# A projection piece taken undivided, read by two engines at one time, and its words split by GpSimd

## The chip, the cores and the metric

The kernel runs on one core of one Trainium2 chip. A core has TensorE (PE, matmuls), VectorE (DVE), ScalarE (ACT), GpSimd (POOL) and SyncE (SP, which here issues DMAs). They run side by side, each in the order of its own queue, and wait for one another by semaphores. Matmuls write PSUM, which VectorE and ScalarE can read. The metric is the time of one execution in microseconds (us); lower is better.

## The reference

The input `x` is 8 sequences of 4096 tokens with 192 channels. Each token becomes a weighted sum of itself and the six before it, with seven softmax weights for each of 8 heads of 24 channels. What comes out goes through a gated network:

```python
out = np.einsum('hk,bskhg->bshg', w, x_unf)     # the convolution, w = softmax(weight)
x = out.reshape(B * S, D)                       # 32768 x 192
gate = np.maximum(x @ w_gate, 0.0)              # 192 -> 1536
val = x @ w_val                                 # 192 -> 1536
return (gate * val @ w_out).astype(np.float32)  # 1536 -> 192
```

## The kernel before, in words

The sequences are taken in two streams, of four sequences each, which lie on partitions 0 to 63 and 64 to 127. The 4 x 4096 tokens of a stream are cut into 16 units of 1024 tokens, and each unit into two windows of 512. The matmuls are in float16, their sums in float32. The order on every engine is the order in which the code is written out; a framework adds the waits.

Unit `u` goes through these steps.

- **Gate and value** (`gate_val`, L534 to L564): for each window, 12 blocks of 128 features. Each block takes two PSUM tiles (gate, value) of 12 matmuls each (L549). ScalarE takes the Relu of the gate (L560), VectorE multiplies it with the value (L561) into `hT`. PSUM is a pool of four tiles of two banks, taken in turn, so a block can start only when the block two before it has been read.
- **Convolution of the next unit.** The part of 576 tokens is VectorE's: ScalarE gives the first of seven products (`lane_first`, L507), VectorE adds six (`lane_rest`, L521). The other 448 tokens are GpSimd's: products for each tap `k` and channel chunk `c` go into the buffer `prods`, of which there is one; ScalarE makes most of them (L491), VectorE the five in the list `VECTOR` (L493). In the following unit GpSimd adds them up, one add for each tap (`add`, L497).
- **Input of the unit after that**: GpSimd reorders loaded tokens (`lane_turn`, L471), SP issues nine transposes of them (L475), and GpSimd issues the next loads (`lane_load`, L207).
- **Projection** (`project_across`, L706, for units 1 to 14). It is computed transposed, output channels on partitions and tokens along the columns, as three pieces: piece 0 and piece 1 are channels 0 to 127 of the two windows, piece 2 is channels 128 to 191 of both. Each piece holds two streams or windows in the two banks of one PSUM tile. [...] A no-operation in SP's queue (`turn_over`, L671) stands between the turns. The order of the passes is (piece 0, turn 0), (2, 0), (0, 1), (1, 0), (2, 1), (1, 1).
- **Out of PSUM.** A float32 is copied as two 16-bit words, low words and high words apart (`words`, L678, its copies in L679), so that 16-bit DMA transposes can turn the planes. SP writes the planes to a DRAM buffer `held` (L739, L744); in the next unit it issues four transposes from there (`turn_back`, L687) and four writes to the output (`send`, L697).

The last pass, (piece 1, turn 1), is divided into two halves of 256 columns:

```python
cross_pass(1, hs, at[1], 1, done[1], slice(0, half))
words(nc.scalar.copy, pt, at[1], both, 0, half)
cross_pass(1, hs, at[1], 1, None, slice(half, WIN))
words(nc.scalar.copy, pt, at[1], slice(0, 1), half, WIN)
words(nc.vector.tensor_copy, pt, at[1], slice(1, 2), half, WIN)
```

Beside this work VectorE makes three of its five products at the end of `lane_rest` (L857), that is before its `words` copy, and the other two after it (L746).

Of the kernel before, what the change touches and what calls it, by code (L numbers as in the profile page):

```python
# [8 lines left out]
FP = mybir.dt.float32  # L9
F16 = mybir.dt.float16  # L10
I32 = mybir.dt.int32
U16 = mybir.dt.uint16
# [5 lines left out]
def kernel(  # L18
# [12 lines left out]
    nc = tc.nc  # L31

    B, S, D = x.shape
# [8 lines left out]
    WIN = 512  # L42
    NWIN = S // WIN
    SUB = 112
    VECTOR = [(0, 5), (1, 5), (2, 5), (0, 6), (2, 1)]
    FOR_POOL = [(1, 6), (2, 6)]
    GSUB = 5
    DSUB = 104
# [3 lines left out]
    NUNIT = NB * S // UNIT  # L52
# [11 lines left out]
    xpool = ctx.enter_context(tc.tile_pool(name="xpool", bufs=2))  # L64
# [3 lines left out]
    ypool = ctx.enter_context(tc.tile_pool(name="ypool", bufs=1))  # L68
# [4 lines left out]
    psum = ctx.enter_context(tc.tile_pool(name="psum", bufs=4, space=bass.MemoryType.PSUM))  # L73
# [442 lines left out]

    def lane_rest(v, now=len(VECTOR)):
        acc = accs.pop(v)
        for k in range(1, KW):
            for c in range(NCH):  # L520
                nc.vector.scalar_tensor_tensor(  # L521
                    out=xc[v][:, c, 0:LDVE] if k == KW - 1 else acc[:, c, :],
                    in0=shifted(v, c, k, 0),
                    scalar=tap[:, c, k : k + 1],
                    in1=acc[:, c, :],
                    op0=ALU.mult,
                    op1=ALU.add,
                )
        if v + 1 < NUNIT:
            prods[v] = apool.tile([128, KW, NCH, LPOOL], FP, name="prods")  # L530
            for c, k in VECTOR[:now]:
                product(nc.vector, v, c, k)
# [108 lines left out]
                flat[:, q0 : q0 + n],  # L641
            )

    across, planes = {}, {}

    def cross_pass(piece, hs, ps, turn, after, cols=slice(0, WIN)):


        for f in range(NFF):
            for r in range(2):  # L650
                bank = r ^ turn
                for half in range(2):
                    if piece == 2:
                        w, st, d = bank, half, 128
                    else:
                        w, st, d = piece, bank, 64 * half
                    mm = nc.tensor.matmul(  # L657
                        out=ps[64 * half : 64 * half + 64, bank, cols],
                        lhsT=Wo[64 * r : 64 * r + 64, f, d : d + 64],
                        rhs=hs[w][64 * r : 64 * r + 64, f, st, cols],  # L660
                        start=(turn == 0 and f == 0),
                        stop=(turn == 1 and f == NFF - 1),
                        tile_position=(64 * r, 64 * half),
                        skip_group_check=True,
                    )
                    if after is not None:
                        tc.add_manual_dep(mm.ins, after.ins.name, SYNC, reason="same banks, other rows")
                        after = None
        return turn_over(turn, mm)
# [5 lines left out]
        tc.add_manual_dep(done.ins, mm.ins.name, SYNC, reason="first turn over")  # L675
        return done

    def words(copy, pt, ps, banks, t0, t1):  # L678
        copy(  # L679
            out=pt[:, banks, :, t0:t1],  # L680
            in_=ps[:, banks, t0:t1].bitcast(U16).rearrange("p b (t l) -> p b l t", l=2),
        )

    def turn_back(u, i):
        w, st = i // 2, i % 2
        os_ = opool.tile([128, 4, D], FP, name="out_s")
        nc.sync.dma_start_transpose(  # L687
            out=os_[:].bitcast(U16),
            in_=planes[u][w, st].rearrange("c (l t) -> (c l) t", l=2),
        )  # L690
        across[u, i] = os_

    def send(u, i):
        w, st = i // 2, i % 2
        bp, w0 = u * UNIT // S, u * UNIT % S // WIN
        row0 = (bp + NB * st) * S + WIN * (w0 + w)
        nc.sync.dma_start(  # L697
            out=bass.AP(
                tensor=out.tensor,
                offset=out.offset + row0 * D,  # L700
                ap=[[D, 128], [128 * D, 4], [1, D]],
            ),
            in_=across.pop((u, i))[:],
        )

    def project_across(u, hs, work):  # L706
        held = planes[u] = dram.tile([2, 2, D, 2 * WIN], U16, name="held")
        at, done = {}, {}
        back = u - 1 in planes
        both, half = slice(0, 2), WIN // 2  # L710
        for i, turn in [(0, 0), (2, 0), (0, 1), (1, 0), (2, 1), (1, 1)]:
            if turn == 0:
                at[i] = psum.tile([128, 2, 512], FP, name="ps")
                done[i] = cross_pass(i, hs, at[i], 0, None)
                if back:
                    if i == 0:
                        turn_back(u - 1, 3)
                    elif i == 2:
                        send(u - 1, 2)
                    else:  # L720
                        send(u - 1, 3)
                continue
            for c, k in work[(0, 2, 1)[i]]:
                product(nc.scalar, u + 1, c, k)
            pool, name = (ypool, "y") if i == 1 else (xpool, "x_h")
            pt = pool.tile([128, 2, 2, WIN], U16, name=name)
            if i == 1:
                cross_pass(1, hs, at[1], 1, done[1], slice(0, half))
                words(nc.scalar.copy, pt, at[1], both, 0, half)
                cross_pass(1, hs, at[1], 1, None, slice(half, WIN))  # L730
                words(nc.scalar.copy, pt, at[1], slice(0, 1), half, WIN)
                words(nc.vector.tensor_copy, pt, at[1], slice(1, 2), half, WIN)
            else:
                cross_pass(i, hs, at[i], 1, done[i])
                words(nc.scalar.copy, pt, at[i], both, 0, WIN)
            flat = pt[:].rearrange("p b l t -> p b (l t)")
            if i == 2:
                for st in range(2):
                    nc.sync.dma_start(  # L739
                        out=held[:, st, 128:D, :].rearrange("w c e -> c w e"),  # L740
                        in_=flat[64 * st : 64 * st + 64],
                    )
            else:
                nc.sync.dma_start(out=held[i, :, 0:128, :].rearrange("s c e -> c s e"), in_=flat)  # L744
        if u + 2 < NUNIT:
            for c, k in VECTOR[3:]:  # L746
                product(nc.vector, u + 1, c, k)

    def project(u, hs, work, y=None):
# [68 lines left out]
    for u in range(NUNIT):  # L818
        adds = 1 <= u < NUNIT - 1
        if u + 1 < NUNIT:  # L820
            xc[u + 1] = xcpool.tile([128, NCH, UNIT], F16, name="xc")
        if adds:
            add(u, 1)
        hs = []
        if u == 0:
            hs.append(gate_val(0, 0))
        if 0 < u < NUNIT - 1:
            load_rest(lane_turn(u + 1))
        if u - 1 in planes:
            turn_back(u - 1, 0)  # L830
            turn_back(u - 1, 1)
            send(u - 1, 0)
            turn_back(u - 1, 2)
            send(u - 1, 1)
            if u == NUNIT - 1:
                turn_back(u - 1, 3)
                send(u - 1, 2)
                send(u - 1, 3)
        if 0 < u < NUNIT - 2:
            load_rest(lane_load(u + 2))  # L840
        if u == 1:
            for c, k in FOR_POOL:
                product(nc.gpsimd, u, c, k)
        if adds:
            for k in range(2, KW):
                add(u, k)
        while len(hs) < 2:
            hs.append(gate_val(u, len(hs)))
        del xc[u]
        work = [[] for _ in range(4)]  # L850
        if u + 1 < NUNIT:
            begun = lane_first(u + 1)
            if u == 0:
                flat = ypool.tile([128, ROOM], F16, name="y")
                y = flat[:, 0 : GSUB * NCH * 128].rearrange("p (j c s r) -> p j c s r", j=GSUB, c=NCH, s=2)
                load_rest(lane_load(2, begun))
            lane_rest(u + 1, len(VECTOR) if u in (0, NUNIT - 2) else 3)  # L857
        if u + 2 < NUNIT:
            todo = [(c, k) for k in (0, 1, 2, 3, 4, 6) for c in range(NCH)]
            todo = [ck for ck in todo if ck not in VECTOR + (FOR_POOL if u == 0 else [])]  # L860
            cuts = [0, 5, 10, 15, 16] if u == 0 else [0, 10, 16, 16]
            work = [todo[a:b] for a, b in zip(cuts, cuts[1:])]
        if 0 < u < NUNIT - 1:
            project_across(u, hs, work)
        else:
            project(u, hs, work, y if u == 0 else None)
        if u == 0:
            conv_turn(2, y)
# [30 lines left out]
```

## Time and profile before

| | |
|---|---|
| median of three runs | 791.49 us (790.75 to 794.97) |
| the profiled execution | 789.98 us |
| its span, first to last instruction | 788.2 us |
| PE busy | 761.1 us, 97% |
| DVE busy | 706.0 us, 90% |
| ACT busy | 630.3 us, 80% |
| POOL busy | 379.9 us, 48% |
| granted TensorE clock | 1.00 |

A row of a group of instructions gives the line, the engine, the operation, the tiles written and read, the shape and the count, then the busy time and the mean of one in ns, then the idle time of that engine just before them and what ended it. A row of the timeline gives start, duration, engine, line and operation; a bracket gives the idle time before it and the releaser. The line of a helper stands for all who call it: L679 is every copy of `words`, and the tile's name tells which (`x_h` for pieces 0 and 2, `y` for piece 1).

### The profile page before, as it was taken

What the parts mean: (1) busy time and instruction counts of PE and PEld (TensorE: products, weight loads), DVE (VectorE), ACT (ScalarE), POOL (GpSimd) and SP (SyncE); (2) the same over time, 40 slices, a digit from 0 to 9 for tenths busy, and PEclk for the clock granted to TensorE, in tenths of its full rate; (3) what the DMA queues carried; (4) which work ended last, traced back from release to release, by engine and by line L of the source; (5) the groups of instructions that cost most, each with busy time, mean ns of one, the idle gap of its engine ahead of it and who ended that gap; (6) DMA issues with size and microseconds to landing.
All of it is one profiled execution on the core that took longest, in us unless ns stands there. A gap on an engine that the chain in (4) does not pass through costs nothing.

```text
span 788.2 us, 31924 instructions
## 1 busy us (share of the span) xinstructions
PE 761.1 (97%) x14295; PEld 504.5 (64%) x14295; DVE 706.0 (90%) x768; ACT 630.3 (80%) x733; POOL 379.9 (48%) x249
## 2 busy tenths in 40 slices
PE   9999999999999999999999999999999999999998
PEld 4495566666666666666666666666666666666548
DVE  7999989899898998989989899898998989999791
ACT  6787978879788797887978879788797887876672
POOL 8529358092561916619165290753908438081000
PEclk9999999999999999999999999999999999999999
DMA  8969039596594965949769496794969939443732
GB/s 114 131 119 129 2 97 153 158 115 141 121 160 141 108 163 105 152 143 117 164 105 147 138 122 159 105 153 131 144 139 119 161 114 146 125 117 92 174 89 82
DMA packets 231313, 100.42 MB, mean 127 GB/s; under 512 B 185288, under 2 KB 220424, under 8 KB 231176
## 3 DMA queue, kind: packets, MB, share of 16 engines
q1 hardware_dynamic: 189928, 82.71, 52.1%
q0 software_dynamic: 41104, 15.57, 20.5%
q8 instruction: 111, 1.82, 1.0%
q14 instruction: 26, 0.21, 0.1%
q10 hardware_dynamic: 144, 0.10, 0.0%
HBM read 31.48 MB, written 47.19 MB: 100 GB/s over the span
## 4 chain that ended last, share of the span: by engine, by line
PE 67%; ACT 26%; issue 2%; DMA 2%; SPq 2%; POOL 0%; ACTq 0%; DVE 0%; POOLq 0%
PE ps L549 59%; ACT prods L491 15%; ACT x_h L679 6%; PE ps L657 4%; ACT acc L507 3%; PE ps L578 3%; ACT y L679 2%; SPq L475 1%; DMA out_s<-held 1%; PE ps L627 1%; DMA x_h<-in_x_dram 0%; PE ps L369 0%; POOL x_p L471 0%; ACTq L491 0%; POOL x_h L133 0%
## 5 line engine op out<-in xcount | busy, mean ns | idle before, releaser
L561 DVE TENSOR_TENSOR hT<-gr,ps 128x1024 f16<-128x1024 f16 (+1 forms) x386 | 467.8, 1216 | 30.3 <-ACT gr L560 6.1
L560 ACT ACTIVATE gr<-ps 128x1024 f16<-128x1024 f32 (+1 forms) x386 | 393.4, 1020 | 104.2 <-PE ps L549 103.2
L497 POOL TENSOR_TENSOR prods<-prods 128x1344 f32<-128x1344 f32 x70 | 212.9, 3042 | 312.5 <-DVE prods L493 309.1
L549 PE MATMUL ps<-xc,Wv 64*64 64x512 f16 (+1 forms) x4320 | 322.8, 376 | 0.3
L549 PE MATMUL ps<-xc,Wg 64*64 64x512 f16 (+1 forms) x4320 | 322.8, 376 | 0.0
L657 PE MATMUL ps<-hT,Wo 64*64 64x512 f16 (+1 forms) x4704 | 223.4, 346 | 22.1 <-ACT y L679 22.1
L549 PEld LDWEIGHTS <-Wv 64*64 64x64 f16 (+1 forms) x4320 | 154.3, 105 | 97.3 <-issue 4.6
L549 PEld LDWEIGHTS <-Wg 64*64 64x64 f16 (+1 forms) x4320 | 157.0, 106 | 89.2 <-issue 0.4
L657 PEld LDWEIGHTS <-Wo 64*64 64x64 f16 x4704 | 157.1, 107 | 88.6 <-issue 24.8
L521 DVE SCALAR_TENSOR_TENSOR acc<-x_r,tap,acc 128x576 f32<-128x576 f16 x225 | 165.3, 815 | 0.0
L491 ACT ACTIVATE prods<-x_r,tap 128x448 f32<-128x448 f16 x222 | 127.4, 662 | 0.0
L679 ACT COPY x_h<-ps 128x2048 uint16<-128x2048 uint16 x28 | 51.9, 1852 | 8.7 <-PE ps L657 8.7
L207 POOL DMA_DIRECT2D x_e<-in_x_dram x58 | 46.9, 818 | 15.4 <-ACT acc L507 11.6
L471 POOL COPY x_p<-x_e 128x960 f16<-128x960 f16 (+1 forms) x58 | 50.5, 912 | 0.5 <-DMA x_e<-in_x_dram 0.4
L497 POOL TENSOR_TENSOR xc<-prods 128x1344 f16<-128x1344 f32 x14 | 42.5, 3038 | 1.1
L679 ACT COPY y<-ps 128x1024 uint16<-128x1024 uint16 (+1 forms) x28 | 22.4, 801 | 22.4 <-PE ps L657 22.4
L679 DVE COPY y<-ps 128x512 uint16<-128x512 uint16 x14 | 9.7, 692 | 30.6 <-ACT y L679 30.6
L521 DVE SCALAR_TENSOR_TENSOR xc<-x_r,tap,acc 128x576 f16<-128x576 f16 x45 | 34.1, 816 | 0.0
L507 ACT ACTIVATE acc<-x_r,tap 128x576 f32<-128x576 f16 x45 | 31.4, 765 | 0.0
L493 DVE TENSOR_SCALAR prods<-x_r,tap 128x448 f32<-128x448 f16 x70 | 27.7, 450 | 0.0
L578 PE MATMUL ps<-Wo,hT 64*128 64x192 f16 x576 | 24.6, 243 | 0.0
L578 PEld LDWEIGHTS <-hT 64*128 64x128 f16 x576 | 23.9, 94 | 0.5
(61 smaller groups left out, 80.4 us busy)
## 6 DMA issues: line engine op xcount, KB each, us to landing
out_dram<-out_s SPq DMA_DIRECT2D x62, 384.0 KB, 3.9
held<-x_h SPq DMA_DIRECT2D x14, 512.0 KB, 2.8
held<-x_h SPq DMA_DIRECT2D x28, 256.0 KB, 3.2
held<-y SPq DMA_DIRECT2D x14, 512.0 KB, 3.3
x_e<-in_x_dram POOLq DMA_DIRECT2D x34, 192.0 KB, 7.5
x_e<-in_x_dram POOLq DMA_DIRECT2D x24, 240.0 KB, 5.2
x_r<-x_p SPq DMA_TRANSPOSE x131, 5.5
out_s<-held SPq DMA_TRANSPOSE x56, 4.5
```

The lines of the kernel that those rows point to most:

```text
L207: first = nc.gpsimd.dma_start(out=xe[:, j0 + start : j0 + n, st, :, :].rearrange("p j c r -> p j (c r)"), in_=bass.AP(tensor=x.tensor, off ...
L471: nc.gpsimd.tensor_copy(out=xp[:, j0 : j0 + n, :, st, :], in_=xe[:, j0 : j0 + n, st, :, :])
L491: engine.activation(out=out, in_=in_, func=ACTF.Copy, scale=scale)
L497: nc.gpsimd.tensor_tensor(out=pr[:, 0] if k < KW - 1 else xc[v + 1][:, :, LDVE:UNIT], in0=pr[:, 0], in1=pr[:, k], op=ALU.add,)
L507: nc.scalar.activation(out=accs[v][:, c, :], in_=shifted(v, c, 0, 0), func=ACTF.Copy, scale=tap[:, c, 0:1],)
L521: nc.vector.scalar_tensor_tensor(out=xc[v][:, c, 0:LDVE] if k == KW - 1 else acc[:, c, :], in0=shifted(v, c, k, 0), scalar=tap[:, c, k : k ...
L549: nc.tensor.matmul(out=pss[i][m : m + M, st, :], lhsT=W[64 * st : 64 * st + 64, c, 128 * f + m : 128 * f + m + M], rhs=xcb[64 * st : 64 * ...
L560: nc.scalar.activation(out=gr[:, sts], in_=pss[0][:, sts], func=ACTF.Relu)
L561: nc.vector.tensor_tensor(out=h[:, f, sts], in0=gr[:, sts], in1=pss[1][:, sts], op=ALU.mult)
L578: mm = nc.tensor.matmul(out=outs[q], lhsT=h[64 * r : 64 * r + 64, f, st, 128 * q : 128 * (q + 1)], rhs=Wo[64 * r : 64 * r + 64, f, :], sta ...
L657: mm = nc.tensor.matmul(out=ps[64 * half : 64 * half + 64, bank, cols], lhsT=Wo[64 * r : 64 * r + 64, f, d : d + 64], rhs=hs[w][64 * r : 6 ...
L679: copy(out=pt[:, banks, :, t0:t1], in_=ps[:, banks, t0:t1].bitcast(U16).rearrange("p b (t l) -> p b l t", l=2),)
```

## The change

- The last pass is no longer divided: it runs over all 512 columns. `cross_pass` loses its column argument and takes, in `ps`, a place for each bank.
- Piece 1 takes two PSUM tiles, not one. The first stream lies in bank 0 of one tile, the second in bank 1 of the other. A unit's projection so takes four PSUM tiles, not three.
- Its two streams are copied as float32 into one tile `raw` of the pool `xpool`, 512 columns by ScalarE and 512 by VectorE; nothing is split into words there. `raw` is a third tenant of the two `x_h` buffers.
- In the next unit, after the reordering of `lane_turn`, GpSimd copies `raw` to the `y` tile as split words (2048 words a partition), and SP then writes the planes to `held`: this write moves from the end of a unit to a place behind the nine transposes of the next.
- The list `VECTOR` begins with (2, 1), which was last, and two products, not three, are made before the copy out of PSUM (`NOW`), three after it.

```diff
-    VECTOR = [(0, 5), (1, 5), (2, 5), (0, 6), (2, 1)]
+    VECTOR = [(2, 1), (0, 5), (1, 5), (2, 5), (0, 6)]
+    NOW = 2
...
                     mm = nc.tensor.matmul(
-                        out=ps[64 * half : 64 * half + 64, bank, cols],
+                        out=ps[bank][64 * half : 64 * half + 64],
                         lhsT=Wo[64 * r : 64 * r + 64, f, d : d + 64],
-                        rhs=hs[w][64 * r : 64 * r + 64, f, st, cols],
+                        rhs=hs[w][64 * r : 64 * r + 64, f, st, :],
...
-    def words(copy, pt, ps, banks, t0, t1):
-        copy(
-            out=pt[:, banks, :, t0:t1],
-            in_=ps[:, banks, t0:t1].bitcast(U16).rearrange("p b (t l) -> p b l t", l=2),
-        )
+    def words(copy, pt, src):
+        copy(out=pt[:], in_=src[:].bitcast(U16).rearrange("p b (t l) -> p b l t", l=2))
+
+    def keep(u, i, pt):
+        flat = pt[:].rearrange("p b l t -> p b (l t)")
+        if i < 2:
+            nc.sync.dma_start(
+                out=planes[u][i, :, 0:128, :].rearrange("s c e -> c s e"), in_=flat
+            )
+            return
+        for st in range(2):
+            nc.sync.dma_start(
+                out=planes[u][:, st, 128:D, :].rearrange("w c e -> c w e"),
+                in_=flat[64 * st : 64 * st + 64],
+            )
...
             if turn == 0:
-                at[i] = psum.tile([128, 2, 512], FP, name="ps")
+                tiles[i] = [psum.tile([128, 2, 512], FP, name="ps") for _ in range(1 + (i == 1))]
+                at[i] = [tiles[i][-n][:, n, :] for n in range(2)]
                 done[i] = cross_pass(i, hs, at[i], 0, None)
...
+            cross_pass(i, hs, at[i], 1, done[i])
             if i == 1:
-                cross_pass(1, hs, at[1], 1, done[1], slice(0, half))
-                words(nc.scalar.copy, pt, at[1], both, 0, half)
-                cross_pass(1, hs, at[1], 1, None, slice(half, WIN))
-                words(nc.scalar.copy, pt, at[1], slice(0, 1), half, WIN)
-                words(nc.vector.tensor_copy, pt, at[1], slice(1, 2), half, WIN)
+                raw = xpool.tile([128, 2, WIN], FP, name="x_h")
+                nc.scalar.copy(out=raw[:, 0, :], in_=at[1][0])
+                nc.vector.tensor_copy(out=raw[:, 1, :], in_=at[1][1])
+                raws[u] = raw
             else:
-                cross_pass(i, hs, at[i], 1, done[i])
-                words(nc.scalar.copy, pt, at[i], both, 0, WIN)
+                pt = xpool.tile([128, 2, 2, WIN], U16, name="x_h")
+                words(nc.scalar.copy, pt, tiles[i][0])
+                keep(u, i, pt)
         if u + 2 < NUNIT:
-            for c, k in VECTOR[3:]:
+            for c, k in VECTOR[NOW:]:
                 product(nc.vector, u + 1, c, k)
...
         if u - 1 in planes:
+            pt = ypool.tile([128, 2, 2, WIN], U16, name="y")
+            words(nc.gpsimd.tensor_copy, pt, raws.pop(u - 1))
+            keep(u - 1, 1, pt)
             turn_back(u - 1, 0)
...
-            lane_rest(u + 1, len(VECTOR) if u in (0, NUNIT - 2) else 3)
+            lane_rest(u + 1, len(VECTOR) if u in (0, NUNIT - 2) else NOW)
```

More of the change, by code (lines that the diff above doesn't have):

```diff
@@ L642, in whole_half, with cross_pass @@
             )
-    across, planes = {}, {}
-    def cross_pass(piece, hs, ps, turn, after, cols=slice(0, WIN)):
+    across, planes, raws = {}, {}, {}
+    def cross_pass(piece, hs, ps, turn, after):
         for f in range(NFF):
@@ L706, in project_across @@
     def project_across(u, hs, work):
[L707 to L710, printed above, removed]
+        planes[u] = dram.tile([2, 2, D, 2 * WIN], U16, name="held")
+        tiles, at, done = {}, {}, {}
         for i, turn in [(0, 0), (2, 0), (0, 1), (1, 0), (2, 1), (1, 1)]:
             if turn == 0:
-                at[i] = psum.tile([128, 2, 512], FP, name="ps")
+                tiles[i] = [psum.tile([128, 2, 512], FP, name="ps") for _ in range(1 + (i == 1))]
+                at[i] = [tiles[i][-n][:, n, :] for n in range(2)]
                 done[i] = cross_pass(i, hs, at[i], 0, None)
-                if back:
+                if u - 1 in planes:
                     if i == 0:
                         turn_back(u - 1, 3)
-                    elif i == 2:
-                        send(u - 1, 2)
                     else:
-                        send(u - 1, 3)
+                        send(u - 1, 2 + (i == 1))
                 continue
@@ L724, in project_across @@
                 product(nc.scalar, u + 1, c, k)
-            pool, name = (ypool, "y") if i == 1 else (xpool, "x_h")
-            pt = pool.tile([128, 2, 2, WIN], U16, name=name)
+            cross_pass(i, hs, at[i], 1, done[i])
             if i == 1:
-                cross_pass(1, hs, at[1], 1, done[1], slice(0, half))
-                words(nc.scalar.copy, pt, at[1], both, 0, half)
-                cross_pass(1, hs, at[1], 1, None, slice(half, WIN))
-                words(nc.scalar.copy, pt, at[1], slice(0, 1), half, WIN)
-                words(nc.vector.tensor_copy, pt, at[1], slice(1, 2), half, WIN)
-            else:
-                cross_pass(i, hs, at[i], 1, done[i])
-                words(nc.scalar.copy, pt, at[i], both, 0, WIN)
[L736 to L744, printed above, removed]
+                raw = xpool.tile([128, 2, WIN], FP, name="x_h")
+                nc.scalar.copy(out=raw[:, 0, :], in_=at[1][0])
+                nc.vector.tensor_copy(out=raw[:, 1, :], in_=at[1][1])
+                raws[u] = raw
+            else:
+                pt = xpool.tile([128, 2, 2, WIN], U16, name="x_h")
+                words(nc.scalar.copy, pt, tiles[i][0])
+                keep(u, i, pt)
         if u + 2 < NUNIT:
-            for c, k in VECTOR[3:]:
+            for c, k in VECTOR[NOW:]:
                 product(nc.vector, u + 1, c, k)
```

## The prediction

> **What bounds the kernel now.** I began with the page: busy shares, the granted clock, then the costliest groups with the idle time before them.
>
> ```profile
> span 788.2 us, 31924 instructions
> PE 761.1 (97%) x14295; PEld 504.5 (64%) x14295; DVE 706.0 (90%) x768; ACT 630.3 (80%) x733; POOL 379.9 (48%) x249
> ...
> L657 PE MATMUL ps<-hT,Wo 64*64 64x512 f16 (+1 forms) x4704 | 223.4, 346 | 22.1 <-ACT y L679 22.1
> ```
>
> TensorE (PE) is busy 97% of the span, and nearly all of the rest is one wait: 22.1 us in which a projection matmul (L657) stands until ScalarE (ACT) has done its `y` copy (L679). So I went to the timeline where a unit's projection meets the next unit. Each row is start, duration, engine, line, operation.
>
> ```profile
> 331.37 14.46 PE L657 MATMUL ps<-hT,Wo 64*64 64x512 f16 x288
> 331.88 2.10 ACT L507 ACTIVATE acc<-x_r,tap 128x576 f32<-128x576 f16 x3
> 333.16 11.02 DVE L521 SCALAR_TENSOR_TENSOR acc<-x_r,tap,acc 128x576 f32<-128x576 f16 x15
> 333.88 5.69 ACT L491 ACTIVATE prods<-x_r,tap 128x448 f32<-128x448 f16 x10
> ...
> 344.10 2.27 DVE L521 SCALAR_TENSOR_TENSOR xc<-x_r,tap,acc 128x576 f16<-128x576 f16 x3
> 344.59 1.85 ACT L679 COPY x_h<-ps 128x2048 uint16<-128x2048 uint16 x1
> 346.28 1.18 DVE L493 TENSOR_SCALAR prods<-x_r,tap 128x448 f32<-128x448 f16 x3
> 346.34 1.01 ACT L679 COPY y<-ps 128x1024 uint16<-128x1024 uint16 x1
> ...
> 347.40 1.50 PE L657 MATMUL ps<-hT,Wo 64*64 64x256 f16 x48 [1.58 <-ACT y L679]
> 348.71 0.84 PE L549 MATMUL ps<-xc,Wg 64*64 64x512 f16 x12
> 348.95 0.59 ACT L679 COPY y<-ps 128x512 uint16<-128x512 uint16 x1 [1.60 <-PE ps L657]
> 349.57 0.69 DVE L679 COPY y<-ps 128x512 uint16<-128x512 uint16 x1 [2.11 <-ACT y L679]
> 349.60 1.02 ACT L560 ACTIVATE gr<-ps 128x1024 f16<-128x1024 f32 x1
> ...
> 350.18 0.81 DVE L493 TENSOR_SCALAR prods<-x_r,tap 128x448 f32<-128x448 f16 x2
> ...
> 350.90 1.22 DVE L561 TENSOR_TENSOR hT<-gr,ps 128x1024 f16<-128x1024 f16 x1
> ...
> 351.30 0.84 PE L549 MATMUL ps<-xc,Wg 64*64 64x512 f16 x12
> 352.17 0.84 PE L549 MATMUL ps<-xc,Wv 64*64 64x512 f16 x12
> ```
>
> The last piece is projected in two column halves. PE does the first, ending at 345.83, then waits 1.58 us because ACT reads that half out of the same PSUM tile from 346.34 to 347.35; only then does the second half run. There is a second, smaller loss: the tile of 12 matmuls that starts at 351.30 is followed by one at 352.17, 0.87 us later instead of about 0.65 (the stage's 31.31 us, below, over 48 tiles). That is the third feature block waiting for the PSUM buffer of the first, which VectorE (DVE) frees at the end of its product at 350.90 + 1.22.
>
> The busy time by stage (length, then PE, its weight loads, DVE, ACT, POOL, and the granted clock, 1.00):
>
> ```profile
> 331.37:348.71 17.34, 15.76 (x340) 11.28 (x336) 16.02 (x23) 15.98 (x23) 0.00 (x0) 1.00 0.40 113
> 348.71:380.02 31.31, 31.29 (x585) 20.34 (x580) 28.76 (x26) 24.56 (x25) 24.92 (x14) 1.00 1.01 141
> ```
>
> So a unit is 17.34 us of projection and 31.31 us of gate and value.
>
> **The change, part by part.**
>
> *Undivided last pass.* What a whole pass costs is read by cutting the window after one, two and five passes:
>
> ```profile
> 331.37 2.79 PE L657 MATMUL ps<-hT,Wo 64*64 64x512 f16 x48
> 331.37 5.38 PE L657 MATMUL ps<-hT,Wo 64*64 64x512 f16 x96
> 331.37 13.15 PE L657 MATMUL ps<-hT,Wo 64*64 64x512 f16 x240
> ```
>
> Each pass adds 2.59 us; the 0.20 us over is the drain of the last matmuls. Six whole passes take 15.54 us, and the next unit would start at 346.91 instead of 348.71: **1.80 us saved** (the wait of 1.58, the drain before it 0.20, and 0.02 of splitting). That needs nobody else to be late at 346.91, so I take each candidate from the rows above.
> - DVE's last write of the next `xc` ends at 344.10 + 2.27 = 346.37. Slack 0.54 us.
> - ACT's copy of the second piece ends at 344.59 + 1.85 = 346.44; its buffer goes to the first value tile, at 346.91 + 0.65 = 347.56. Slack 1.1 us.
> - The two raw copies replace the three `y` copies. 512 elements take ACT 0.59 and DVE 0.69 us in those rows. They start when the pass has drained, 346.91 + 0.20 + 0.05 (348.90 to 348.95 now) = 347.16; DVE has by then done its two products (1.18 x 2/3 after 346.28 is 347.07). ACT ends at 347.75, DVE at 347.85. Their buffers go to the second feature block, at 346.91 + 1.30 = 348.21. Slack 0.35 us, the smallest.
> - ACT starts its first Relu 0.89 us after the unit's start (349.60 against 348.71), here 347.80; the raw copy is done 0.05 us before.
>
> *The stall in the third block.* DVE now does the raw copy and three products, not two, ahead of its first product of gate and value. By the rows, a copy moves it on by 0.61 us (349.57 to 350.18) and a product by 0.36 (350.18 to 350.90 is two): 347.16 + 0.61 + 1.08 = 348.85, 1.94 us after the unit's start against 2.19 now. Its product then ends at 346.91 + 3.16, and the third block's value tile is due at 346.91 + 3.24. So that stall (0.22 us) just goes; between 0 and 0.22 I take 0.22, since the Relu that the product also waits for (347.80 + 1.02) is as early.
>
> *GpSimd (POOL).* It gets one new copy of 2048 two-byte elements a unit, and starts each unit earlier. Its rows in two units,
>
> ```profile
> 302.51 3.04 POOL L497 TENSOR_TENSOR prods<-prods 128x1344 f32<-128x1344 f32 x1 [23.11 <-DVE prods L493]
> ...
> 326.02 3.04 POOL L497 TENSOR_TENSOR xc<-prods 128x1344 f16<-128x1344 f32 x1
> ...
> 351.16 3.04 POOL L497 TENSOR_TENSOR prods<-prods 128x1344 f32<-128x1344 f32 x1 [22.10 <-DVE prods L493]
> 354.14 3.46 POOL L471 COPY x_p<-x_e 128x960 f16<-128x960 f16 x4
> ...
> 373.66 3.04 POOL L497 TENSOR_TENSOR xc<-prods 128x1344 f16<-128x1344 f32 x1
> ```
>
> and, by groups, with the mean of one in ns behind the bar and the busy time:
>
> ```profile
> L471 POOL COPY x_p<-x_e 128x960 f16<-128x960 f16 x30 | 28.8, 988 | 0.3 <-DMA x_e<-in_x_dram 0.3
> ...
> L493 POOL TENSOR_SCALAR prods<-x_r,tap 128x448 f32<-128x448 f16 x2 | 2.8, 1432 | 0.0
> ```
>
> Its first add waits for DVE's product (2, 1), which is now the last of the five and moves to the first: it can start at about 346.8, the unit's start, not 2.45 us after it. From 351.16 to 376.70 POOL needs 25.5 us; from 302.51 to 329.06, in a unit that begins a sequence of the input, 26.5. What it must be done by: ACT overwrites the single `prods` buffer 2.51 us into the next projection (333.88), which is 31.08 + 2.51 = 33.6 us after the unit's start. That leaves 8.1 us for the new copy, or 7. At the rate of its copies (988 ns for 960) it takes 2.1 us, at that of its slowest row (1432 ns for 448) 6.5 us. The operation is a copy, so I take 2.1; either is covered, at no cost. If the cover were gone, each us over 7 costs PE one.
>
> [...]
>
> *DVE beside POOL.* More POOL work lies beside DVE. DVE's product in the 12.5 us with POOL adding, and in the 4 us with POOL idle:
>
> ```profile
> L561 DVE TENSOR_TENSOR hT<-gr,ps x11: 1220/1222/1222, 312.6 to 325.5; 128x1024 f16<-128x1024 f16 x11
> ...
> L561 DVE TENSOR_TENSOR hT<-gr,ps x4: 1221/1221/1222, 328.1 to 332.0; 128x1024 f16<-128x1024 f16 x4
> ```
>
> No difference, so nothing is charged. [...]
>
> *Queues.* The write of the third piece to DRAM leaves SP at the boundary and stands behind the nine transposes of the next unit, with a wait for POOL's copy; behind it are the four transposes back and the sends.
>
> ```profile
> 356.08 14.65 SPq L475 DMA_TRANSPOSE x_r<-x_p  x9
> ...
> 378.01 0.53 SPq L697 DMA_DIRECT2D out_dram<-out_s  x1
> ```
>
> and by DMA, with the median us from issue to landing:
>
> ```profile
> held<-x_h SPq DMA_DIRECT2D x14, 512.0 KB, 2.8
> ```
>
> The transposes end at 370.7, 22 us into the unit; POOL's copy would be done by 3.0 + 3.5 + 6.5 = 13. The write adds 0.4 us of issue and lands some 3 us later, before the third transpose back (376). SP's next duty to PE is the end of the projection's first pass, 380.02 + 2.59 = 382.6, 4 us after its last send. Cost 0, and if SP came later than that, PE would wait by as much. The raw tile takes a buffer of the `x_h` pair, whose first piece is issued at 341.4 and lands 2.8 us later, 3 us before 347.16: 0.
>
> **The sum.** 1.80 + 0.22 = 2.02 us at 13 boundaries; a unit would be 48 tiles of 0.6475 and six passes, 31.08 + 15.54 = 46.62 us with PE never waiting. Unit 14 has neither products nor the second stall:
>
> ```profile
> 720.49 14.46 PE L657 MATMUL ps<-hT,Wo 64*64 64x512 f16 x288
> ...
> 737.95 0.82 PE L549 MATMUL ps<-xc,Wg 64*128 64x512 f16 x6
> ```
>
> 17.46 us, of which 0.1 is the switch to wider tiles that stays: 1.8 saved. 13 x 2.02 + 1.8 = 28.1 us. The profiled execution took 789.98 us (span 788.2 and 1.8 around it), so 761.9; the median of the runs is 1.5 above the profiled one, so **763 us**.
>
> **Rivals.**
> - *The wait only moves.* For it: now DVE's `y` copy starts only when ACT's ends (2.11 <-ACT y). If the raw copies also went one behind the other, DVE's would end at 347.75 + 0.69 = 348.44, 0.25 us past need, and its first product at 348.44 + 1.0 + 1.2 = 350.65, some 0.5 past it. Against: the copies read separate tiles and write separate halves, and both wait for the same earlier ACT instruction. 13 x 0.5 to 0.75 us comes back: 769 to 773.
> - *GpSimd becomes the bound (slower).* Over 7 us for its copy, ACT's products start late; 0.54 us of that is slack, and 2.02 us the gain, so from about 9.5 us (4.6 ns an element) the kernel is slower. At 11 us, 13 x 1.5 = 19 us: 811. For it: two-byte elements four bytes apart, a form that the trace lacks. Against: the rows give 1.0 to 3.2 ns. From 6.3 us, POOL's last add would also reach into L521 (333.16, 31.08 + 1.79 after the start); if an L521 waited for a whole add, PE would lose 3.04 - 0.54 = 2.5 us, 0.48 over the gain: 13 x 0.48 more than 790, 796; I give that 0.01 of this rival's chance. [...]
> - *Nothing gained.* The granted clock falls once PE has no gaps: 4% would eat it all, 790. Against: 1.00 in both windows above, one of them 31 us with PE busy throughout.
>
> **How the numbers follow.** Forecast 759 to 768 (the low end is the sum without the median's 1.5 us and with 0.2 us a boundary for drains counted too long; the high end keeps the third block's stall, 2.9 us, and 0.15 us a boundary): 0.78. Moved wait: 0.10. Nothing gained: 0.05. Slower: 0.07. Faster is the first two, 0.88. A half per cent, 4 us, the spread of the three runs before (790.75 to 794.97), is about what a measurement can tell from no change. The range, 759 to 773, takes the forecast and the moved wait.
>
> **What would show it.** Right: no wait of L657 for a copy, 46.6 us from unit to unit, raw copies of 0.59 and 0.69 us starting together, POOL's first add at the unit's start, its new copy of 2 to 6.5 us, PE busy over 99%. Wrong: idle time before L549's first blocks put down to DVE or ACT copies, the new GpSimd copy over 7 us, L521 over 815 ns, or a granted clock under 1.

## The result and the profile after

The changed kernel takes 830.61 us (median of four runs, 829.84 to 832.17) against 791.12 us of the kernel before: 4.9% slower, ratio 1.0492 with a 95% interval of 1.0453 to 1.0531. The forecast was 763 us.

The page of the changed kernel, in the lines that answer to those of before:

```profile
span 828.1 us, 30624 instructions
PE 781.6 (94%) x13623; PEld 493.2 (60%) x13623; DVE 750.8 (91%) x768; ACT 616.8 (74%) x719; POOL 413.7 (50%) x263
...
PEclk9999999999999998999999999998999999999999
...
L494 DVE TENSOR_SCALAR prods<-x_r,tap 128x448 f32<-128x448 f16 x70 | 72.6, 1088 | 0.0
```

and its list of waits:

```profile
PE ps L550 <- DVE hT L562: 42.4, 13, 3.3
```

The wait of the projection for a copy is gone, as meant. In its place the gate and value matmuls wait 42.4 us for VectorE's product, 13 times, once at each boundary but the last. And one group has changed its duration: VectorE's products for the convolution (L494, before L493) take 1088 ns on average, not 450. The instruction is the same one.

The timeline of one boundary, in the columns of the prediction's:

```profile
411.71 3.44 PE L658 MATMUL ps<-hT,Wo 64*64 64x512 f16 x60
412.14 2.27 DVE L522 SCALAR_TENSOR_TENSOR xc<-x_r,tap,acc 128x576 f16<-128x576 f16 x3
...
414.33 0.81 DVE L494 TENSOR_SCALAR prods<-x_r,tap 128x448 f32<-128x448 f16 x2
...
414.92 3.11 POOL L498 TENSOR_TENSOR prods<-prods 128x1344 f32<-128x1344 f32 x1 [24.19 <-DVE prods L494]
414.95 0.84 PE L550 MATMUL ps<-xc,Wg 64*64 64x512 f16 x12
415.24 0.69 DVE L737 COPY x_h<-ps 128x512 f32<-128x512 f32 x1
415.27 0.59 ACT L736 COPY x_h<-ps 128x512 f32<-128x512 f32 x1 [0.79 <-ACT x_h L680]
...
415.84 4.62 DVE L494 TENSOR_SCALAR prods<-x_r,tap 128x448 f32<-128x448 f16 x3
...
417.54 0.84 PE L550 MATMUL ps<-xc,Wg 64*64 64x512 f16 x12
417.97 3.94 POOL L472 COPY x_p<-x_e 128x960 f16<-128x960 f16 x4
...
420.38 2.33 DVE L562 TENSOR_TENSOR hT<-gr,ps 128x1024 f16<-128x1024 f16 x2
421.64 1.35 PE L550 MATMUL ps<-xc,Wv 64*64 64x512 f16 x12 [3.25 <-DVE hT L562]
...
422.71 1.56 PE L550 MATMUL ps<-xc,Wg 64*64 64x512 f16 x12
...
425.26 0.85 PE L550 MATMUL ps<-xc,Wg 64*64 64x512 f16 x12
```

Up to 415.84 everything is as forecast: the next unit follows the projection at once, and the two raw copies run side by side in 0.69 and 0.59 us. Then the three products behind the raw copy take 4.62 us in place of 1.1. The line's own view for this stretch has their spread (shortest, median and longest of the five, in ns; two of them stand ahead of the raw copy):

```profile
L494 DVE TENSOR_SCALAR prods<-x_r,tap x5: 449/1167/2440, 414.3 to 419.3; 128x448 f32<-128x448 f16 x5
```

The first of the three, 2440 ns, ends at 418.28, just behind the end of GpSimd's add (414.92 + 3.11 = 418.03); the other two, 1167 ns each, lie beside GpSimd's reorder copies, which take about as long one by one (3.94 for four). So VectorE's first product of gate and value starts at 420.38 and not at 416.9, and the value tile due at 417.54 + 0.65 = 418.19 starts at 421.64.

What follows the wait is a second loss, seen in the windows view (length, PE busy, granted clock):

```profile
421.64:425.20 3.56, 3.56 (x36) 0.53 0.37 74
```

The mean granted clock of the stretch is 0.53: for 3.4 us of it the clock is 0.5, and a tile of 12 matmuls takes about 1.28 us. By the trace's record of the clock this happens at all 13 boundaries, for 3.41 us at eleven of them and for 6.8 us at two.

A unit so takes 51.75 us (the chain of waits has projections that start at 399.61 and 451.36): the forecast's 46.62, 3.45 us of lateness (421.64 - 418.19) and the 1.68 us that are left, which the half clock explains (half of 3.41 is 1.71). 13 x 5.13 = 66.7 us on the forecast's 761.9 is 828.6; the profiled execution took 829.84. The two units with 6.8 us at half clock are longer, 53.0 us (294.81 to 347.83 in the chain of waits).

### The profile page after: what moved, and what is told of

Its sections match the earlier page's. It is cut to its first block, busy times and chain, and to the rows that moved or that the text cites. A ratio compares the mean times of both kernels' runs of the same rounds, so it can differ in the third digit from the quotient of the medians.

```text
span 828.1 us, 30624 instructions
## 1 busy us (share of the span) xinstructions
PE 781.6 (94%) x13623; PEld 493.2 (60%) x13623; DVE 750.8 (91%) x768; ACT 616.8 (74%) x719; POOL 413.7 (50%) x263
## 4 chain that ended last, share of the span: by engine, by line
PE 93%; DVE 5%; issue 1%; DMA 0%; POOL 0%; ACT 0%; DVEq 0%; POOLq 0%
PE ps L550 62%; PE ps L658 26%; DVE prods L494 4%; PE ps L579 3%; DVE hT L562 2%; PE ps L628 1%; DMA x_h<-in_x_dram 0%; PE ps L370 0%; POOL x_h L134 0%; PE ps L411 0%; ACT acc L605 0%; DVEq L562 0%; POOL steps L133 0%; POOLq L133 0%; POOLq L884 0%
## 5 line engine op out<-in xcount | busy, mean ns | idle before, releaser
L561 ACT ACTIVATE gr<-ps 128x1024 f16<-128x1024 f32 (+1 forms) x386 | 392.9, 1019 | 169.2 <-PE ps L550 167.2
L498 POOL TENSOR_TENSOR prods<-prods 128x1344 f32<-128x1344 f32 x70 | 215.4, 3077 | 321.4 <-DVE prods L494 318.1
L550 PE MATMUL ps<-xc,Wv 64*64 64x512 f16 (+1 forms) x4320 | 335.2, 390 | 42.4 <-DVE hT L562 42.4
L550 PE MATMUL ps<-xc,Wg 64*64 64x512 f16 (+1 forms) x4320 | 333.6, 388 | 0.0
L550 PEld LDWEIGHTS <-Wv 64*64 64x64 f16 (+1 forms) x4320 | 157.8, 109 | 147.3 <-issue 57.0
L658 PE MATMUL ps<-hT,Wo 64*64 64x512 f16 x4032 | 220.2, 376 | 0.0
L658 PEld LDWEIGHTS <-Wo 64*64 64x64 f16 x4032 | 139.5, 107 | 78.0
L522 DVE SCALAR_TENSOR_TENSOR acc<-x_r,tap,acc 128x576 f32<-128x576 f16 x225 | 165.3, 813 | 0.0
L494 DVE TENSOR_SCALAR prods<-x_r,tap 128x448 f32<-128x448 f16 x70 | 72.6, 1088 | 0.0
L472 POOL COPY x_p<-x_e 128x960 f16<-128x960 f16 (+1 forms) x58 | 56.6, 1013 | 1.7 <-DMA x_e<-in_x_dram 1.7
L680 POOL COPY y<-x_h 128x2048 uint16<-128x2048 uint16 x14 | 26.6, 1900 | 29.9 <-ACT x_h L736 29.9
L522 DVE SCALAR_TENSOR_TENSOR xc<-x_r,tap,acc 128x576 f16<-128x576 f16 x45 | 34.1, 814 | 0.0
L736 ACT COPY x_h<-ps 128x512 f32<-128x512 f32 x14 | 8.2, 588 | 10.9 <-ACT x_h L680 6.3
```

The costliest lines, as they stand in the source:

```text
L472: nc.gpsimd.tensor_copy(out=xp[:, j0 : j0 + n, :, st, :], in_=xe[:, j0 : j0 + n, st, :, :])
L494: engine.tensor_scalar(out=out, in0=in_, scalar1=scale, scalar2=None, op0=ALU.mult)
L498: nc.gpsimd.tensor_tensor(out=pr[:, 0] if k < KW - 1 else xc[v + 1][:, :, LDVE:UNIT], in0=pr[:, 0], in1=pr[:, k], op=ALU.add,)
L522: nc.vector.scalar_tensor_tensor(out=xc[v][:, c, 0:LDVE] if k == KW - 1 else acc[:, c, :], in0=shifted(v, c, k, 0), scalar=tap[:, c, k : k ...
L550: nc.tensor.matmul(out=pss[i][m : m + M, st, :], lhsT=W[64 * st : 64 * st + 64, c, 128 * f + m : 128 * f + m + M], rhs=xcb[64 * st : 64 * ...
L561: nc.scalar.activation(out=gr[:, sts], in_=pss[0][:, sts], func=ACTF.Relu)
```

## The experiments

Where no range of times is given, a kernel was run once; four runs of one kernel lay within 0.7% of each other.

**The order put back.** First the suspect by itself: `VECTOR` in its old order, all else of the change kept.

```diff
-    VECTOR = [(2, 1), (0, 5), (1, 5), (2, 5), (0, 6)]
+    VECTOR = [(0, 5), (1, 5), (2, 5), (0, 6), (2, 1)]
```

> The changed kernel with (2, 1) put back to the end of VECTOR; all else of the change stays, so GpSimd's first add again starts only behind the last of VectorE's products. Theory (VectorE's three products after the raw copy are held up by GpSimd's first add and reorder copies, which start too early): the products go back to 0.45 us each, the 3.25 us wait of the third block's value tile goes, the clock stays at 1.00, and the time is the sum of the prediction, 762 to 764 us. Rival (the raw copies, the extra PSUM tile or GpSimd's new copy are to blame): the time stays at 825 to 832.

Measured: 761.92 us (761.64 to 762.5), ratio to the kernel before 0.9639, interval 0.9623 to 0.9655, clock 1.00. The timeline of one boundary of this kernel:

```profile
382.46 0.81 DVE L494 TENSOR_SCALAR prods<-x_r,tap 128x448 f32<-128x448 f16 x2
...
383.10 0.83 PE L550 MATMUL ps<-xc,Wg 64*64 64x512 f16 x12
383.37 0.69 DVE L737 COPY x_h<-ps 128x512 f32<-128x512 f32 x1
383.40 0.59 ACT L736 COPY x_h<-ps 128x512 f32<-128x512 f32 x1 [0.79 <-ACT x_h L680]
...
383.98 1.17 DVE L494 TENSOR_SCALAR prods<-x_r,tap 128x448 f32<-128x448 f16 x3
...
385.06 5.09 DVE L562 TENSOR_TENSOR hT<-gr,ps 128x1024 f16<-128x1024 f16 x4
...
385.32 3.04 POOL L498 TENSOR_TENSOR prods<-prods 128x1344 f32<-128x1344 f32 x1 [19.64 <-DVE prods L494]
...
391.68 1.91 POOL L680 COPY y<-x_h 128x2048 uint16<-128x2048 uint16 x1
```

GpSimd's add now starts behind the third product, and the three take 1.17 us together. The windows view over one unit shows TensorE without a gap:

```profile
367.74:414.37 46.63, 46.63 (x869) 29.35 (x864) 44.84 (x49) 39.59 (x47) 26.66 (x15) 1.00 0.83 145
```

So the whole loss hangs on the order of the list, and the rest of the change gains what it was forecast to gain.

**Only GpSimd's start held.** Is it the order, or the time at which GpSimd comes in? The changed kernel's order stays; the first add gets a wait for VectorE's last product.

```diff
...
+        if k == 1:
+            tc.add_manual_dep(one.ins, latest[v].ins.name, SYNC, reason="behind the last product")
```

> The changed kernel, order of VECTOR and all, with one wait added: GpSimd's first add of a unit waits for VectorE's last product. Theory: as with the order put back, 762 to 765 us, which says that it is the time at which GpSimd starts, not the order of the products. Rival (the order of the products itself, through what they wait for): 825 to 832.

Measured: 763.17 us, clock 1.00, and the products (L496 here, by groups) are back:

```profile
L496 DVE TENSOR_SCALAR prods<-x_r,tap 128x448 f32<-128x448 f16 x70 | 27.6, 447 | 0.0
```

It is the time at which GpSimd starts.

**The order alone, in the kernel before.**

```diff
-    VECTOR = [(0, 5), (1, 5), (2, 5), (0, 6), (2, 1)]
+    VECTOR = [(2, 1), (0, 5), (1, 5), (2, 5), (0, 6)]
```

> The kernel before with nothing changed but VECTOR, (2, 1) first. Theory: GpSimd's first add starts some 4 us earlier, beside VectorE's third product (some 2.9 us in place of 0.36), and its reorder copies beside the last two (1.17 us each); the first product of gate and value ends near 354.3 on the clock of the profile before, the third block's value tile was due at 351.95: 2.2 us more a unit at 13 boundaries, 819 us, and up to 841 if the clock falls in the longer wait. Rival (the order harmless, the rest of the change to blame): 788 to 795.

Measured: 800.4 us (799.05 to 804.09), ratio 1.0131, interval 1.0104 to 1.0158, clock 1.00 (0.998 in the longest run). Slower, as the theory says, but by 10 us where it said 28 or more: both ranges missed, and the third product is not held up. Its timeline:

```profile
351.39 1.17 DVE L493 TENSOR_SCALAR prods<-x_r,tap 128x448 f32<-128x448 f16 x3
...
351.98 3.47 POOL L497 TENSOR_TENSOR prods<-prods 128x1344 f32<-128x1344 f32 x1 [22.04 <-DVE prods L493]
...
355.27 1.53 DVE L493 TENSOR_SCALAR prods<-x_r,tap 128x448 f32<-128x448 f16 x2
...
355.39 3.80 POOL L471 COPY x_p<-x_e 128x960 f16<-128x960 f16 x4
...
357.99 0.84 PE L549 MATMUL ps<-xc,Wv 64*64 64x512 f16 x12 [0.75 <-DVE hT L561]
```

Here GpSimd is the one that waits: its add shows 3.47 us, 0.43 more than its 3.04, and VectorE's three products, one close behind the other, keep their time. The last two start at 355.27, when the add is nearly over (355.45); together they take 1.53 us, the time of one free product (0.36 to the next) and one of 1.17 beside a reorder copy. 0.75 us at 13 boundaries is the 10 us lost. So in this kernel the products hold up the add, where in the changed kernel the add held up a product. One guess is that there the raw copy between the products let the add in; the experiment *Who gets in* tests it.

**The new copy doubled.** GpSimd's word copy, made twice in the changed kernel.

```diff
-            words(nc.gpsimd.tensor_copy, pt, raws.pop(u - 1))
+            for _ in range(2):
+                words(nc.gpsimd.tensor_copy, pt, raws[u - 1])
```

> The changed kernel with GpSimd's word copy made twice in each unit (same source, same target). Theory: the copy lies beside products of gate and value, which it doesn't slow, and GpSimd has some 8 us to spare: 829 to 833, no change against the changed kernel. Rival (the new copy on GpSimd is what holds VectorE up): 13 times 1.9 us more, about 855.

Measured: 829.69 us. Twice the copy (3.85 us) and the same wait of TensorE, from the timeline and the list of waits:

```profile
421.45 1.36 PE L550 MATMUL ps<-xc,Wv 64*64 64x512 f16 x12 [3.25 <-DVE hT L562]
421.67 3.85 POOL L680 COPY y<-x_h 128x2048 uint16<-128x2048 uint16 x2
```

The new work on GpSimd is not to blame, only when GpSimd's old work begins.

**What in the product is held up.** The products in another form of the operation, which also sums its output; the sum is thrown away.

```diff
-            engine.tensor_scalar(out=out, in0=in_, scalar1=scale, scalar2=None, op0=ALU.mult)
...
+                engine.tensor_scalar(out=out, in0=in_, scalar1=scale, scalar2=0.0, op0=ALU.mult, op1=ALU.add, accum_out=spare[:])
```

> The changed kernel with VectorE's products in the form of the operation that also sums up its output (the sum is thrown away), an instruction that takes longer by itself. [...] If every VectorE read of memory is held up by GpSimd, the products beside it stay at 1.2 to 2.4 us or more: 830 or above.

Measured: 774.97 us, clock 1.00. The form takes 675 ns, and the extra instruction that reads out the sum (83 ns) runs beside the next one. The line's view over the whole run, and one boundary:

```profile
L498 DVE TENSOR_SCALAR_CACHE_REDUCE prods<-x_r,tap x70: 666/675/680, 55.3 to 677.5; 128x448 f32<-128x448 f16 x70
```

```profile
389.62 3.04 POOL L502 TENSOR_TENSOR prods<-prods 128x1344 f32<-128x1344 f32 x1 [20.60 <-DVE prods L498]
...
391.19 0.68 DVE L498 TENSOR_SCALAR_CACHE_REDUCE prods<-x_r,tap 128x448 f32<-128x448 f16 x1
```

666 to 680 ns, beside GpSimd's add and away from it. A slower form of the same product, with the same reads and the same early add, makes the changed kernel 55 us faster; what it still loses against 761.92 us are mostly 13 waits of 0.8 us for VectorE, whose products are now slower. So it isn't VectorE's reading of SBUF, the memory in which these tiles lie, in general that GpSimd holds up, but something that the plain form has and this one hasn't. The two differ in speed as well: the plain form makes 448 elements in 450 ns, where 576 of L522 take 814 ns and 448 of this form 675. Whether that has to do with it, no run shows. What the runs show is that either engine can be the one held up: a product took 2440 ns behind an add, and an add 3.47 us behind products. The recorded starts don't always tell which it will be, as the next experiment shows.

**Who gets in.** (2, 1) third of the five, so that three products follow the raw copy without a gap and GpSimd comes free after the first of them.

```diff
-    VECTOR = [(2, 1), (0, 5), (1, 5), (2, 5), (0, 6)]
+    VECTOR = [(0, 5), (1, 5), (2, 1), (2, 5), (0, 6)]
```

> The changed kernel with (2, 1) third in VECTOR, so first of the three products behind the raw copy; GpSimd's first add comes free while VectorE goes straight from one product to the next. [...] Theory B (GpSimd gets its turn between any two instructions): the last product takes about 2.9 us, the third block waits 2.3 us or more at 13 boundaries, 792 us, or some 815 with a lower clock.

Measured: 816.69 us, clock 0.977, the time that theory B gave with a lower clock. The timeline:

```profile
409.69 3.94 DVE L494 TENSOR_SCALAR prods<-x_r,tap 128x448 f32<-128x448 f16 x3
...
410.30 3.08 POOL L498 TENSOR_TENSOR prods<-prods 128x1344 f32<-128x1344 f32 x1 [23.87 <-DVE prods L494]
...
414.81 0.84 PE L550 MATMUL ps<-xc,Wv 64*64 64x512 f16 x12 [2.58 <-DVE hT L562]
```

The second of these products takes its usual 447 ns, and the third, next to it, 3218: here the add came in between two products that stand one behind the other, which it did not do in the reordered kernel before. In both kernels the add starts some 0.1 us before the product in question (here 410.30 against 409.69 + 2 x 0.36 = 410.41, there 351.98 against 351.39 + 2 x 0.36 = 352.11), and one product lost and the other won. So the guess fell: a gap in VectorE's work isn't needed to let the add in. Theory B is no rule either, since in the reordered kernel before the add did not get its turn between two products. What decides so near a tie stays open. What the loser pays does not: the third product ends at 409.69 + 3.94 = 413.63, 0.25 us behind the add's end (410.30 + 3.08 = 413.38), as the first one behind the raw copy did in the changed kernel (418.28 against 418.03), and the add behind the products took 0.43 us more than its 3.04.

**A shorter wait.** Four products ahead of the raw copy, one behind it, in the changed kernel.

```diff
-    NOW = 2
+    NOW = 4
```

> The changed kernel with four products ahead of the raw copy and one behind it. The raw copy starts 0.8 us later, 347.95; GpSimd's add takes over in that gap and the one product behind it ends at about 351.2, the first product of gate and value at 352.4, due at 350.15 to 350.5: a wait of about 2.0 us in place of 3.25, or 0.4 and 2.0 in two pieces. If the fall of the clock comes only with waits longer than these: clock 1.00, 788 to 793 us. If any wait of this kind brings it: clock 0.97, about 812.

Measured: 787.58 us, clock 1.00. The timeline:

```profile
394.49 1.53 DVE L494 TENSOR_SCALAR prods<-x_r,tap 128x448 f32<-128x448 f16 x4
...
395.07 3.84 POOL L498 TENSOR_TENSOR prods<-prods 128x1344 f32<-128x1344 f32 x1 [20.64 <-DVE prods L494]
...
396.54 2.62 DVE L494 TENSOR_SCALAR prods<-x_r,tap 128x448 f32<-128x448 f16 x1
...
400.34 0.84 PE L550 MATMUL ps<-xc,Wv 64*64 64x512 f16 x12 [1.53 <-DVE hT L562]
```

One product is held up until the add's end (395.07 + 3.84 = 398.91), and the wait is 1.53 us, shorter than the 2.0 expected, which puts the time just under the range. The add itself shows 3.84 us, 0.80 over its 3.04: it started beside the four products in a row, which end at 394.49 + 1.53 = 396.02.

The clock stays at 1.00: it fell at all 13 boundaries with waits of 3.25 us, at 11 of 13 with 2.58, and at none with 1.53. In the record of the clock, all falls of one kernel begin on one grid with steps of 3.413 us, and the half clock lasts one step (3.41 us) or two (6.8). In these traces the falls go with the work of TensorE in one step of the grid. Two boundaries of the kernel of *Who gets in*, cut along its grid (length, PE busy, granted clock):

```profile
463.73:467.15 3.42, 1.25 (x24) 1.00 0.00 0
467.15:470.56 3.41, 3.41 (x39) 0.50 0.35 71
...
514.93:518.35 3.42, 1.37 (x28) 1.00 0.02 5
518.35:521.76 3.41, 3.41 (x71) 1.00 0.30 58
```

In that kernel and the changed one, from 60 to 770 us, the clock fell behind every step with 1.25 us of work or less, 24 of them, and behind none with 1.37 us or more. With one product behind the raw copy, no stretch of 3.41 us has less than 1.87 us of work.

**The undivided pass alone.** The kernel before, its last pass whole, in one PSUM tile, its words split by ScalarE.

```diff
-                cross_pass(1, hs, at[1], 1, done[1], slice(0, half))
-                words(nc.scalar.copy, pt, at[1], both, 0, half)
-                cross_pass(1, hs, at[1], 1, None, slice(half, WIN))
-                words(nc.scalar.copy, pt, at[1], slice(0, 1), half, WIN)
-                words(nc.vector.tensor_copy, pt, at[1], slice(1, 2), half, WIN)
+                cross_pass(1, hs, at[1], 1, done[1])
+                words(nc.scalar.copy, pt, at[1], both, 0, WIN)
```

> The kernel before with the last pass undivided and nothing else: one PSUM tile, and ScalarE splits all its words in one copy of 1.85 us. The pass saves 1.80 us; the copy runs from 347.16 to 349.0 on the clock of the profile before, the first Relu follows at 349.0, the first product of gate and value ends at 351.3 and the third block's value tile was due at 350.15: 1.2 us come back, of which 0.22 were lost before too. 0.8 us saved at 13 boundaries: about 779 us. If the split between two engines and GpSimd were needed for any gain: 788 to 793.

Measured: 777.94 us (776.98 to 778.95), ratio 0.9832, interval 0.9816 to 0.9849. Close to the 779 worked out: some 13 us come from not dividing the pass. The other 16 (777.94 to 761.92) go with ScalarE's copy: in the trace it takes 1.86 us, the first Relu stands behind it, and VectorE's first product of gate and value waits 1.79 us for that. The rest of the change takes this away (two engines, two tiles, GpSimd's split, two products ahead and not three); its parts were not run apart.

**How much cover GpSimd has.** With the order put back, the word copy made three and five times (`range(3)` and `range(5)` in the edit of the doubled copy).

> The kernel with (2, 1) back at the end of VECTOR, and GpSimd's word copy made three times in a unit. There GpSimd begins 2.2 us after the unit's start and has done its last add 29.2 us after it; ScalarE overwrites its products 33.6 us after the start and VectorE's two-input chain (L522) begins at 32.9. Two more copies are 3.8 us: the last add ends at 33.0. Theory of the prediction (3.7 to 4.4 us of cover): 762 to 764 us. If the cover is smaller than reckoned: each us late costs 13 us.

> The same with the word copy made five times: 7.6 us more, the last add ends at 36.8, 3.2 us after ScalarE wants the buffer and 3.9 into VectorE's chain of L522. By the buffer alone, ScalarE is 3.2 us late, of which 0.5 is slack: 2.7 us at 13 boundaries, 797 us, L522 at 0.81 us throughout. If L522, with two inputs in SBUF, is held up by GpSimd's reads as the product of one input was: one or two L522 of some 2.5 us or more in each unit, and 797 to 815.

Measured: 766.22 us with three copies, above the 762 to 764 expected, and 806.62 us with five, clock 1.00. The two-input chain L522 in the two kernels, by line:

```profile
L522 DVE SCALAR_TENSOR_TENSOR acc<-x_r,tap,acc x225: 802/806/2230, 42.7 to 710.5; 128x576 f32<-128x576 f16 x113
```

```profile
L522 DVE SCALAR_TENSOR_TENSOR acc<-x_r,tap,acc x225: 802/805/3593, 42.4 to 750.6; 128x576 f32<-128x576 f16 x113
```

With three copies 4 us are lost, no more than runs of one kernel can differ by, but the trace shows delays: three instructions of L522 take 2.12 to 2.23 us, up to 1.4 more than alone, and ScalarE waits three times for GpSimd's adds, 2.3 us in all. With five, single instructions of L522 take up to 3.59 us, 2.8 more than alone; the long ones lie beside GpSimd's last adds, as at one boundary, where four take 6.65 us (fifteen took 11.02 in the trace before):

```profile
389.66 6.65 DVE L522 SCALAR_TENSOR_TENSOR acc<-x_r,tap,acc 128x576 f32<-128x576 f16 x4
390.81 3.42 POOL L498 TENSOR_TENSOR xc<-prods 128x1344 f16<-128x1344 f32 x1
```

So the cover was about what had been reckoned for this kernel, or somewhat less, and L522, with two inputs in SBUF, is held up by GpSimd as well, which the plain duration of 806 ns would not have told. 806.62 lies in the middle of that theory's range; ScalarE waits 46.3 us for GpSimd beside it, and the two were not told apart.

## Why the prediction was wrong

- *Undivided last pass, 1.80 us.* Right. Six passes take 15.54 us in the chain of the changed kernel, and the next unit follows without a wait. The four slacks held too: the raw copies took 0.59 and 0.69 us and nobody waited for them.
- *The stall in the third block.* The sum holds where the products take their free time: with the order put back VectorE's first product of gate and value starts 1.96 us after the unit (385.06 - 383.10; forecast 1.94), and the stall is gone. In the changed kernel three products in front of it took 4.62 us where 1.08 had been summed.
- *GpSimd.* The new copy took 1.90 us (taken: 2.1, bounds to 6.5) and was hidden. That the first add could start at the unit's start was right to 0.1 us (414.92 against 414.95). But the early start was booked as cover only; what the add would now lie beside was not asked.
- *DVE beside POOL: the step that failed.* "No difference, so nothing is charged" rested on L561 alone. The runs show a charge: one product of 2440 ns and two of 1167 in place of 450, which with the fall of the clock cost 5.13 us a unit. The products were not considered, and in the trace before they could not have shown it: GpSimd's add waited for the last of them, so the two never met. The rows did set them apart, with 0.36 us from one product to the next at 448 elements, against 11.02 / 15 = 0.73 for 576 of L521; that this is why they are held up was not shown.
- *Queues.* Right: with the order put back no wait for SP is left, and the unit is 46.63 us long.
- *The rivals.* The slower one had GpSimd holding up VectorE in the wrong place, through its tail, from 6.3 us of copy; such delays exist (L522 of up to 2230 ns with three copies and 3593 with five) but not in the changed kernel (808 to 820 ns). No run shows the term of its 796 us, an L521 that waits for a whole add; the longest L522 took 2.8 us more than alone. The clock rival had the wrong cause: the clock fell behind gaps, not for want of them, and took a third of the 5.13 us a unit.
- *The sum.* 761.9 us was the time of this change without its reordered list: 761.92 measured. The missing term was 13 x 5.13 us.

## What to carry to other kernels

A dependence that makes an engine start late can also be what keeps two engines apart: before moving it, list every instruction that will newly lie beside the one set free, and look for each of them at both engines' durations, not at the commonest one. Here a product (450 ns, up to 3218 beside an add) and the two-input L522 (806 ns, up to 3593) were held up, and another form of the product (675 ns) was not: the duration alone does not tell which. A trace in which two engines never overlap says nothing on the price of their meeting. And a wait of a few us on TensorE can cost more than its length: here 3.25 us cost 1.7 more in clock, 1.53 us cost none.

## What was not expected of the hardware

A plain VectorE product of 450 ns took 2440 and 3218 ns when a GpSimd add of 3.04 us had begun before it, and 1167 ns beside GpSimd copies of about 1 us, while a slower form of it (675 ns) was not touched. Where products went first, GpSimd's add showed 3.47 and 3.84 us. The two-input L522, 806 ns alone, took up to 3593 ns beside GpSimd's adds. The half clock came in pieces of 3.41 us on a fixed grid, behind each step of it, from 60 to 770 us of two kernels, in which TensorE had worked for 1.25 us or less, and behind none with 1.37 us or more; an idle time of 2.58 us was enough at 11 of 13 boundaries.
